# The end of a three-part kernel on one Trainium2 core: order of the last combine rows, place of their transposes, and form of the last product

## The chip, the cores and the metric

The program runs on one core of a Trainium2 chip. Its engines are TensorE (PE: products and transposes into PSUM), VectorE (DVE), ScalarE (ACT), GpSimd (POOL), SyncE (SP, which issues DMAs) and 16 DMA engines. The metric is the device time of one execution in microseconds (us).

## What is computed

Three parts follow one another: a linear attention, a mixture of experts in which every token goes to one expert with a fixed capacity, and a soft mixture of experts. The change touches the end of the third part alone. With x of shape 4352 x 128, 32 slots and 8 experts (F = 1024):

```python
logits = x @ phi
d = np.exp(logits - logits.max(0)); d /= d.sum(0) + 1e-09
slot_input = (d.T @ x).reshape(8, 4, 128)
for e in range(8):
    h = np.maximum(slot_input[e] @ w1[e], 0.0)
    slot_out[e] = h @ w2[e]
c = np.exp(logits - logits.max(1)); c /= c.sum(1) + 1e-09
return c @ slot_out.reshape(32, 128)
```

So every token needs its own row of c (a softmax over 32 slots), and the 32 slot outputs need the logits of all tokens.

## The kernel before, in words

The tokens stand in expert order in x2T (128 features by 4352 slots). The third part takes them in groups of four chunks of 128 slots while the second part still runs; the last group has three chunks and waits for the last expert. `soft_in` (L1277) does one group. Its inner functions are `logits` (PE, L1285), `largest` (DVE L1290 and L1292, ACT exponentials L1297 and L1299), `rows` (PE transposes of x2T L1305, ACT copy L1307), `weights` (PE L1313, ACT es L1317), `sums` (PE L1322, DVE S4 L1325) and `combine` (L1330 to L1352): an ACT copy, a PE transpose, six DVE operations with an ACT exponential between them make c_c, and POOL scatters one chunk at a time into cd in device memory, in token order (L1347). For the last group the order in the code is logits, largest, rows, soft_max, weights, sums and, last, combine (L1366 to L1375); the ACT copy of combine is put behind es by hand (`after`, L1334).

The program is written with a framework that orders the instructions of each engine itself, by their place in the code and by when their inputs are due; `after` adds an order by hand.

`soft_out` (L1447) then makes the slot outputs. slotP (L1459) holds the slot inputs. The first layer (L1469) is 16 products of 512 columns, each for 32 output columns, on the float32 weights M1; ACT and DVE apply the relu (L1473, L1474); eight transposes (L1479) and two copies (L1483, L1485) make HT. The second layer (L1493) is 64 products of 128 columns. A plain float32 product is two PE instructions, called passes here. Its generator `rows_back` (L1535) loads cd back in token order with three DMAs on SP (L1542 to L1544), transposes it in three batches (L1549) and splits each into c_hi, rounded to float32r (ACT, L1552), and the rest c_lo (DVE, L1553). The batches are issued ahead of steps 5, 6 and 7 of the second layer (BACK = 5, L1489). Y is copied out (L1497), Sel puts the slots in order (L1501), and SO is built: block-diagonal over four chunks (a quad), 128 x 512, one tile rounded to float32r and one with the rest (L1505 to L1515). The SO tiles were set to zero by POOL much earlier (L1409, 165.9 us). The last product has, for each of nine quads, three passes of 512 columns in float32r (L1518 to L1520); ACT or DVE copies the result (L1523, L1525), and SP stores it (L1528, 256 KB; the leftover quad 8, which comes first, L1531, 128 KB in pieces of 512 bytes).

`busy` (L1380) issues products of ones (wz) that nothing reads; BUSY holds their numbers, and BUSY[3] = 8 are issued ahead of the first layer (L1461).

Of the kernel before, what the change touches and what calls it, by code (L numbers as in the profile page):

```python
# [33 lines left out]
LS = 2.0 ** -40       # scale of the logits in the assignment  # L34
# [3 lines left out]
CE = 224  # slots of an expert that are filled early  # L38
CL = CAP - CE
TE = 24   # chunks whose tokens may go there  # L40
NE, NL = E * CE // 128, E * CL // 128
SPARE = 4608 + TE     # rows of x; further ones of c take slots that have no token
# [8 lines left out]
class K:  # L51
    def __init__(s, ctx, tc, I, out, dbg=None):
# [3 lines left out]
        s.nl = s.p.tile([128, NCH, 8], F32, name="nl")     # -logits * LS  # L56
        s.bad = s.p.tile([128, 1], I32, name="bad")
        s.badf = s.p.tile([128, 1], F32, name="badf")
        # of every slot, the row of its token for the gather, and the one that it is scattered to
# [11 lines left out]
    # ------------------------------------------------------------ constants  # L71
    def consts(s):
# [9 lines left out]
        # bm[p, h] = (p // 32 == h)  # L82
# [6 lines left out]
    # ------------------------------------------------------------ loads  # L89
# [3 lines left out]
    def after(s, b, a):  # L93
        """orders b behind a on their engine"""
        s.tc.add_manual_dep(b.ins, a.ins.name, mybir.DependencyInfo(
            mybir.DependencyClass.NoSync, mybir.DependencyReason.DATA), reason="order")

    def warm(s, n):
        """keeps the tensor engine busy until the first inputs are there, so that its clock is up"""
# [10 lines left out]
    def fill(s, key, ps):  # L110
        """keeps the tensor engine's clock up while it waits for what goes to this bank"""
# [30 lines left out]
    def x3(s, n, t):  # L142
        """[128 tokens, 4 heads, 32] of chunk t"""
# [4 lines left out]
    def xq(s, n, qd, h):  # L148
        """[128 tokens, (4 chunks, 32)] of a quad and head"""
# [4 lines left out]
    # ------------------------------------------------------------ S1, S2  # L154
    def decode(s):
# [11 lines left out]
        v.tensor_tensor(t[0], t[0], t[2], op=OP.bitwise_and)          # bits of the high part  # L167
# [5 lines left out]
        s.SS = c.tile([8, 2, 2, 4, 32], F32, name="SS")   # [r, hi|rem, S1|S2, rep, d]  # L173
# [4 lines left out]
    def weights(s):  # L178
        """block diagonal pieces of S1, S2 (transposed), and of P = S2^T S2"""
# [9 lines left out]
        hl = c.tile([128, 2, 64], F32, name="hl")        # (h, S1|S2, r)  # L189
# [14 lines left out]
    def pieces(s, r, n, pool=None):  # L204
        """r * 2^21 in two float16 parts, and r itself as bfloat16"""
# [34 lines left out]
    # ------------------------------------------------------------ K, V  # L240
    def ksplit(s, g):
        """K in float16: grid 2^-7, and the rest * 2^21 in two parts"""
# [35 lines left out]
    def phi(s, ph, ab, n):  # L278
        """products of the first n on the vector engine, of the others on Pool"""
# [8 lines left out]
    def add(s, b, h, c, w, x):  # L288
        """accumulates on columns c of a batch and head; the first one clears them all"""
# [29 lines left out]
    # ------------------------------------------------------------ G -> W, KV -> blocks  # L319
    def fin_tiles(s):  # L320
        nc = s.nc
        # pieces of W, block-diagonal over the chunks of a quad: batch b at 136 b, [(c', d), (h, c, r)];
        # so the leftover chunks find their blocks (c = b) 144 apart
        s.W = [s.a.tile([128, 576], dt, name="Wb%d" % i) for i, dt in enumerate((F16, F16, F16, BF))]
        # of a batch and a pair of heads u, rows (h % 2, f): block-diagonal KV, and KV @ w_gate, in columns
        # (u = 0: KV 64) (u = 0: 8) (u = 1: 8) (u = 1: KV 64)
# [6 lines left out]
    def Wof(s, x, qd, h):  # L333
        """the block of a quad and head"""
# [5 lines left out]
    def gfin(s, b):  # L340
        """W = S1 G P of a batch and every head, scaled by 2^-9, in pieces"""
# [3 lines left out]
        # Y = X + X^T, X = K0'R + R'R/2 (scaled by 2^21)  # L345
# [16 lines left out]
        # T1^T [d, (h, r)]  # L362
# [14 lines left out]
        # W^T [(c', d), (h, r)]  # L377
# [21 lines left out]
    def kvfin(s, b):  # L399
        """KV (scaled by 2^-9) of a batch, and KV @ w_gate, for pairs of heads"""  # L400
# [833 lines left out]
    def LO(s, e):  # L1234
        """the engines for the rests of an expert's weights"""
        return s.nc.vector, s.nc.gpsimd
# [488 lines left out]
```

## Time and profile before

| what | us |
|---|---|
| runs: lowest, median, highest of 3 | 316.4, 317.76, 329.15 |
| the profiled execution: span | 320.7 |
| its own time beside the span | not given by the page |
| PE busy | 278.7 (87%) |
| DVE, ACT, POOL busy | 215.0, 158.9, 153.4 |
| stores: first issue, last issue | 308.06, 315.09 |

The span goes from the first to the last instruction of the profiled execution. Busy time is a sum over instructions that may overlap: passes on PE are pipelined, and the share says little about the last 30 us, which are a tenth of it. They are read by windows and by the chain of work that ended last.

### The profile page before, as it was taken

The numbers are of one execution on the slowest core, as the hardware profiler recorded it, in microseconds if no ns is written. First come the engines' busy times: TensorE is split into PE (matmuls) and PEld (weight loads), VectorE is DVE, ScalarE is ACT, GpSimd is POOL, SyncE is SP. The second block draws the span as 40 slices with busy tenths as digits, with TensorE's granted clock in tenths as the row PEclk, the third lists the DMA queues.
The fourth block names the chain that finished last, engine by engine and source line by source line (L and its number), as shares of the span: only waits on it lengthen the run. The fifth ranks groups of instructions, "written<-read, shape, count | busy, mean of one in ns | idle before, by whom it ended". The sixth has DMA issues, their size and how long they took to land.

```text
span 320.7 us, 7215 instructions
## 1 busy us (share of the span) xinstructions
PE 278.7 (87%) x2687; PEld 231.0 (72%) x2697; DVE 215.0 (67%) x726; ACT 158.9 (50%) x457; POOL 153.4 (48%) x194
## 2 busy tenths in 40 slices
PE   7698659988999569999899999999969998999791
PEld 3576547866968548848798989788859997864570
DVE  8988987794593796456587888286655677644240
ACT  3326526543545372343855566468654876532230
POOL 6745434471170161077990505677884864443000
PEclk9759998996798755569999999999997999999977
DMA  6876864000010000128971000123146244200234
GB/s 158 237 252 208 260 192 141 2 36 35 4 65 33 35 1 0 68 82 251 330 231 42 8 3 11 41 52 97 47 145 195 76 141 138 68 8 10 72 132 156
DMA packets 34352, 32.58 MB, mean 102 GB/s; under 512 B 5740, under 2 KB 29284, under 8 KB 34308
## 3 DMA queue, kind: packets, MB, share of 16 engines
q1 hardware_dynamic: 26964, 24.43, 24.8%
q10 hardware_dynamic: 5024, 4.22, 4.6%
q0 software_dynamic: 2320, 3.38, 3.8%
q8 instruction: 23, 0.38, 0.5%
q14 instruction: 21, 0.17, 0.2%
HBM read 26.27 MB, written 5.75 MB: 100 GB/s over the span
## 4 chain that ended last, share of the span: by engine, by line
PE 63%; DVE 19%; POOL 5%; issue 4%; ACT 4%; DMA 2%; ACTq 1%; POOLq 0%; SPq 0%
PE py L1161 6%; PE ph L1151 6%; PE pt L534 4%; PE pt L481 4%; PE ph L1248 3%; PE py L1259 3%; PE ph L1249 3%; PE ph L1250 3%; PE py L1260 2%; PE py L1258 2%; PE acc L291 2%; PE mm L269 2%; PE ph L1171 2%; PE tp L534 2%; POOL cd L1347 2%
## 5 line engine op out<-in xcount | busy, mean ns | idle before, releaser
L1347 POOL DMA_INDIRECT cd<-c_c,ids x34 | 33.9, 998 | 28.5 <-DVE c_c L1345 18.4
L1123 POOL DMA_INDIRECT xg<-xd,idx x34 | 33.2, 977 | 12.7 <-issue 6.9
L1252 DVE SCALAR_TENSOR_TENSOR hl<-ph,hh 128x320 fp32r<-128x320 f32 x64 | 29.1, 486 | 13.5 <-ACT hh L1251 13.2
L1151 PE MATMUL ph<-xe,r 128*128 128x224 f32 x128 | 33.1, 358 | 1.8 <-ACT he L1153 1.5
L1161 PE MATMUL py<-he,r 128*128 128x224 f32 x128 | 34.0, 361 | 0.0
L1153 ACT ACTIVATE he<-ph 128x224 f32<-128x224 f32 x64 | 21.9, 357 | 22.6 <-PE ph L1151 18.9
L1251 ACT ACTIVATE hh<-ph 128x320 fp32r<-128x320 f32 x64 | 25.7, 449 | 7.9 <-PE ph L1250 7.8
L1151 PEld LDWEIGHTS ph<-xe,r 128*128 128x128 f32 x128 | 23.2, 190 | 2.8 <-ACT he L1153 2.1
L1161 PEld LDWEIGHTS py<-he,r 128*128 128x128 f32 x128 | 22.7, 191 | 1.5 <-issue 1.2
L1259 PE MATMUL py<-hh,w2l 128*128 128x320 f32 x64 | 20.5, 320 | 3.2 <-POOL w2l L1112 3.2
L1112 POOL TENSOR_TENSOR w2l<-r,w2h 128x512 fp32r<-128x512 f32 (+1 forms) x20 | 21.7, 1112 | 2.6 <-ACT w2h L1111 2.5
L1248 PE MATMUL ph<-xh,w1h 128*128 128x320 f32 x64 | 21.3, 341 | 0.3 <-ACT xh L1227 0.3
L534 PE MATMUL pt<-KX,phT 128*128 128x72 f32 x120 | 21.4, 327 | 0.0
L1260 PE MATMUL py<-hl,w2h 128*128 128x320 f32 x64 | 20.2, 316 | 1.2 <-DVE hl L1252 1.2
L1250 PE MATMUL ph<-xh,w1l 128*128 128x320 f32 x64 | 20.7, 324 | 0.0
L1249 PE MATMUL ph<-xl,w1h 128*128 128x320 f32 x64 | 20.4, 319 | 0.0
L1258 PE MATMUL py<-hh,w2h 128*128 128x320 f32 x64 | 20.3, 318 | 0.0
L534 PEld LDWEIGHTS pt<-KX,phT 128*128 128x128 f32 x120 | 19.3, 236 | 0.5 <-ACT phT L484 0.2
L467 POOL TENSOR_TENSOR Ahl<-al,l 128x128 f32<-128x128 f32 x9 | 5.7, 635 | 26.5 <-DVE al L466 23.5
L481 PE MATMUL pt<-ident,ph 128*128 128x128 f32 x72 | 16.1, 366 | 1.4 <-POOL ph L283 0.8
L283 POOL TENSOR_TENSOR ph<-kab 128x640 f32<-128x640 f32 x9 | 12.5, 1391 | 10.1 <-ACT kab L272 9.8
L1259 PEld LDWEIGHTS py<-hh,w2l 128*128 128x128 f32 x64 | 12.0, 188 | 4.2 <-POOL w2l L1112 3.6
(454 smaller groups left out, 838.8 us busy)
## 6 DMA issues: line engine op xcount, KB each, us to landing
r<-in_moe_w_dram SPq DMA_DIRECT2D x24, 512.0 KB, 5.0
r<-in_moe_w_dram ACTq DMA_DIRECT2D x8, 512.0 KB, 7.8
xd<-xt SPq DMA_DIRECT2D x9, 256.0 KB, 2.0
kb<-in_k_dram SPq DMA_DIRECT2D x4, 512.0 KB, 7.4
vb<-in_v_dram SPq DMA_DIRECT2D x4, 512.0 KB, 4.7
qb<-in_q_dram SPq DMA_DIRECT2D x4, 512.0 KB, 3.7
out_dram<-ot SPq DMA_DIRECT2D x8, 256.0 KB, 3.3
cd<-on POOLq DMA_DIRECT2D x1, 576.0 KB, 5.0
```

The source lines that it names most:

```text
L481: nc.tensor.transpose(ps[:, 128 * i:128 * i + 128], ph[:, 4 * i + 2 * u:4 * i + 2 * u + 2].rearrange("p h i j -> p (h i j)"), s.ident)
L534: s.lastx = nc.tensor.matmul(ps[:, o:o + 72], s.PHT[qd][:, u, 128 * (2 * k + i):128 * (2 * k + i) + 128], s.KX[:, s.batch(t), 72 * u:72 * ...
L1123: o = nc.gpsimd.indirect_dma_start(out=g, out_offset=None, in_=s.xd[0:rows], in_offset=bass.IndirectOffsetOnAxis(ap=s.idx[:, a:a + 1], axi ...
L1151: o = nc.tensor.matmul(ps, s.RW[e][0][:, 128 * k:128 * k + 128], X[:, CE * e:CE * e + CE], start=True, stop=True)
L1161: o = nc.tensor.matmul(Y[e], s.RW[e][1][:, k], Hs[e][:, k], start=(k == 0), stop=(k == 7))
L1248: nc.tensor.matmul(ps, w1h[:, f], xh, start=True, stop=False)
L1249: nc.tensor.matmul(ps, w1h[:, f], xl, start=False, stop=False)
L1250: nc.tensor.matmul(ps, w1l[:, f], xh, start=False, stop=True)
L1252: nc.vector.scalar_tensor_tensor(hl[:, k], ps, 0.0, hh[:, k].bitcast(F32), op0=OP.max, op1=OP.subtract)
L1258: nc.tensor.matmul(py, w2h[:, f], hh[:, k], start=(k == 0), stop=False)
L1259: nc.tensor.matmul(py, w2l[:, f], hh[:, k], start=False, stop=False)
L1347: st = nc.gpsimd.indirect_dma_start(out=s.cd, out_offset=bass.IndirectOffsetOnAxis(ap=s.ids[:, a:a + 1], axis=0), in_=cc[:, i], in_offset= ...
```

## The change

For the last group, combine comes first, right behind the logits, with no order by hand. BUSY[3] is 6. `rows_back` is an ordinary function that is called behind the second layer, Sel and the scaling of the slot outputs; it keeps the transposed c as plain float32 in one tile c_T. SO and its zeroing go. The slot outputs are written as so, 128 rows by two blocks of 128 columns; odd is 1 where a row belongs to the block. The last product is two plain float32 products per quad, rows 0 to 63 and rows 64 to 127, each 256 columns, into two PSUM tiles; ACT copies the first, DVE the second. The quads go in order 0 to 8. (The change also drops comments.)

```diff
@@ soft_in
         else:
+            combine(s.php.tile([128, CL], F32, name="ph"))
             x = largest()
             rows(x)
             s.busy(s.BUSY[0])
             s.soft_max(new)
-            x = weights(s.php.tile([128, CL], F32, name="ph"))
+            weights(s.php.tile([128, CL], F32, name="ph"))
             s.busy(s.BUSY[1])
             sums()
             s.busy(s.BUSY[2])
-            combine(bank(), x)
-    BACK = 5
-    BUSY = (2, 2, 4, 8, 3)
+    BUSY = (2, 2, 4, 6)
@@ slot_consts
-        zero = [nc.gpsimd.tensor_scalar(x, s.wz, 0.0, 0.0, op0=OP.mult, op1=OP.mult) for x in s.SO]
-        for o in zero + [nc.gpsimd.memset(s.slotP, 0.0)]:
-            s.after(o, s.lastp)
+        s.after(nc.gpsimd.memset(s.slotP, 0.0), s.lastp)
+        s.odd = s.p.tile([128, 2], F32, name="odd")
+        v.tensor_tensor(s.odd, s.bm[:, 0:2], s.bm[:, 2:4], op=OP.add)
@@ soft_out
-        back = s.rows_back()
         for k in range(8):
-            if k >= s.BACK:
-                next(back)
...
-        nc.scalar.activation(Y, py[:, 0:256].rearrange("p (g d) -> p g d", g=2), AF.Copy)
-        ch, cl = s.cT
+        nc.scalar.activation(Y[:, 0], py[:, 0:128], AF.Copy)
+        v.tensor_copy(Y[:, 1], py[:, 128:256])
...
-        sh, sl = tl("s_sh", [128, 128], F32R), tl("s_sl", [128, 128], F32R)
-        nc.scalar.activation(sh, po[:, 0:128], AF.Copy)
...
-        for i, qd in enumerate((8, 0, 1, 2, 3, 4, 5, 6, 7)):
-            pq = s.php.tile([128, 512], F32, name="po")
-            nc.tensor.matmul(pq, ch[:, qd], s.SO[0], start=True, stop=False)
-            nc.tensor.matmul(pq, cl[:, qd], s.SO[0], start=False, stop=False)
-            nc.tensor.matmul(pq, ch[:, qd], s.SO[1], start=False, stop=True)
+        so = tl("s_so", [128, 2, 128])
+        v.tensor_tensor(so, po[:, None, 0:128].to_broadcast([128, 2, 128]),
+                        s.odd[:, :, None].to_broadcast([128, 2, 128]), op=OP.mult)
+        s.rows_back()
+        for qd in range(9):
             ot = s.op.tile([128, 512], F32, name="ot")
-            if i % 2 == 0:
-                nc.scalar.activation(ot, pq, AF.Copy)
-            else:
-                v.tensor_copy(ot, pq)
+            for u in range(2):
+                pq = s.php.tile([128, 512], F32, name="po")
+                r, o = slice(64 * u, 64 * u + 64), ot[:, 256 * u:256 * u + 256]
+                nc.tensor.matmul(pq[:, 0:256], s.cT[r, qd], so[r].rearrange("p j d -> p (j d)"), start=True,
+                                 stop=True)
+                if u == 0:
+                    nc.scalar.activation(o, pq[:, 0:256], AF.Copy)
+                else:
+                    v.tensor_copy(o, pq[:, 0:256])
@@ rows_back
-            nc.scalar.activation(ch[:, g:g + n], o, AF.Copy)
-            v.tensor_tensor(cl[:, g:g + n], o, ch[:, g:g + n].bitcast(F32), op=OP.subtract)
-            yield
+            if n > 2:
+                nc.scalar.activation(s.cT[:, g:g + 2], o[:, 0:2], AF.Copy)
+                v.tensor_copy(s.cT[:, g + 2:g + n], o[:, 2:n])
+            else:
+                nc.scalar.activation(s.cT[:, g:g + n], o, AF.Copy)
```

## Rows read from the trace of the kernel before

**Rows 1.** Windows of the end: busy us (instructions) by engine, PE clock, DMA share, GB/s.

```profile
303.20:305.40 2.20, 0.74 (x5) 0.55 (x5) 0.74 (x4) 1.27 (x4) 0.00 (x0) 1.00 0.00 0
...
307.20:309.30 2.10, 2.10 (x6) 1.66 (x5) 0.69 (x1) 0.75 (x2) 0.00 (x0) 0.50 0.00 0
309.30:313.50 4.20, 4.18 (x18) 3.03 (x16) 2.07 (x3) 1.63 (x3) 0.00 (x0) 0.99 0.95 326
313.50:320.70 7.20, 0.00 (x0) 0.00 (x0) 0.01 (x1) 0.60 (x1) 0.00 (x0) 0.69 0.36 131
```

**Rows 2.** The chain of work that ended last: start us, us, what.

```profile
291.08 0.27 DVE c_c L1345
...
294.18 2.37 DMA cd<-c_c,ids
...
296.69 3.11 DMA c_tok<-cd
...
301.14 0.59 PE po L1549 x4
...
302.56 0.62 PE py L1493 x16
...
303.63 0.73 PE tp L1501 x4
...
305.37 0.50 PE po L1518
```

**Rows 3.** Timeline around the last group: start us, us, engine, line, operation, idle before.

```profile
285.04 0.45 PE L1384 MATMUL ph<-wz 128*128 128x320 bf16 x2
...
285.23 0.44 ACT L1264 ACTIVATE x2T<-py 128x320 f32<-128x320 f32 x1 [2.78 <-PE py L1260]
...
286.85 0.36 ACT L1297 ACTIVATE et<-tp,sN 96x128 f32<-96x128 f32 x1 [1.18 <-DVE sN L1292]
...
289.24 0.26 DVE L1337 TENSOR_REDUCE c_mx<-tp 128x3 f32<-128x96 f32 x1
...
289.96 1.46 PE L1384 MATMUL po<-wz 128*128 128x512 bf16 x6
...
290.56 0.19 DVE L1459 TENSOR_TENSOR slotP<-tp,s_rs 128x32 f32<-128x32 f32 x1
```

**Rows 4.** Timeline of the two layers on PE.

```profile
291.35 3.64 PE L1469 MATMUL po<-r,slotP 128*32 128x512 f32 x32
...
296.32 2.39 PE L1493 MATMUL py<-r,s_HT 128*32 128x128 f32 x80
```

**Rows 5.** Groups of instructions: count, busy us, mean ns, idle before and its releasers.

```profile
L456 DVE TENSOR_TENSOR qab<-mm,l 128x256 f32<-128x256 f32 x9 | 3.7, 416 | 2.5 <-ACT l L452 2.5
...
L1473 ACT ACTIVATE s_H<-po 128x256 f32<-128x256 f32 x2 | 0.8, 384 | 4.6 <-PE po L1469 4.6
...
L1505 ACT ACTIVATE s_sh<-tp 128x128 fp32r<-128x128 f32 x1 | 0.3, 277 | 0.8 <-PE tp L1501 0.8
...
L1409 POOL TENSOR_SCALAR SO<-wz 128x512 fp32r<-128x512 bf16 x2 | 1.4, 710 | 0.0
...
L1347 POOL DMA_INDIRECT cd<-c_c,ids x34 | 33.9, 998 | 28.5 <-DVE c_c L1345 18.4 <-issue 6.7 <-PE ph L1250 2.2
```

**Rows 6.** Timeline of PE amid the early experts, float32 of 224 columns.

```profile
188.35 0.54 PE L1151 MATMUL ph<-xe,r 128*128 128x224 f32 x2
188.72 0.54 PE L1161 MATMUL py<-he,r 128*128 128x224 f32 x2
```

**Rows 7.** Timeline of SP's queue at the stores.

```profile
308.06 0.66 SPq L1531 DMA_DIRECT2D out_dram<-ot  x1
...
313.53 1.46 SPq L1528 DMA_DIRECT2D out_dram<-ot  x1
```

**Rows 8.** Short windows at the stores; the last three columns are PE clock, DMA share, GB/s.

```profile
309.40:309.60 0.20, 0.20 (x3) 0.16 (x2) 0.00 (x0) 0.20 (x1) 0.00 (x0) 1.00 0.79 192
...
315.80:316.20 0.40, 0.00 (x0) 0.00 (x0) 0.00 (x0) 0.00 (x0) 0.00 (x0) 1.00 1.05 374
...
317.20:317.40 0.20, 0.00 (x0) 0.00 (x0) 0.00 (x0) 0.00 (x0) 0.00 (x0) 0.50 0.08 31
```

More of the change, by code (lines that the diff above doesn't have):

```diff
@@ L1328, in sums, with combine @@
                 v.tensor_copy(s.S4[:, 0:129], pS[:, 0:129])
-        def combine(pc, behind=None):
+        def combine(pc):
             l2 = tl("l2", [128, 128])
-            x = nc.scalar.activation(l2[:m], ps[:m, 0:128], AF.Copy)
-            if behind:
-                s.after(x, behind)
+            nc.scalar.activation(l2[:m], ps[:m, 0:128], AF.Copy)
             l3 = turn(l2, pc)
@@ L1502, in soft_out @@
                              start=(g == 0), stop=(g == 1))
-        sh, sl = tl("s_sh", [128, 128], F32R), tl("s_sl", [128, 128], F32R)
-        nc.scalar.activation(sh, po[:, 0:128], AF.Copy)
-        for j in range(4):
-            r, w = slice(32 * j, 32 * j + 32), slice(128 * j, 128 * j + 128)
-            if j < 2:
-                nc.scalar.activation(s.SO[0][r, w], sh[r], AF.Copy)
-            else:
-                v.tensor_copy(s.SO[0][r, w], sh[r])
-        v.tensor_tensor(sl, po[:, 0:128], sh.bitcast(F32), op=OP.subtract)
-        for j in range(4):
-            r, w = slice(32 * j, 32 * j + 32), slice(128 * j, 128 * j + 128)
-            v.tensor_copy(s.SO[1][r, w], sl[r])
-        for i, qd in enumerate((8, 0, 1, 2, 3, 4, 5, 6, 7)):
-            pq = s.php.tile([128, 512], F32, name="po")
-            nc.tensor.matmul(pq, ch[:, qd], s.SO[0], start=True, stop=False)
-            nc.tensor.matmul(pq, cl[:, qd], s.SO[0], start=False, stop=False)
-            nc.tensor.matmul(pq, ch[:, qd], s.SO[1], start=False, stop=True)
-            ot = s.op.tile([128, 512], F32, name="ot")
-            if i % 2 == 0:
-                nc.scalar.activation(ot, pq, AF.Copy)
-            else:
-                v.tensor_copy(ot, pq)
+        so = tl("s_so", [128, 2, 128])
[3 more added lines that the diff above has]
+        for qd in range(9):
+            ot = s.op.tile([128, 512], F32, name="ot")
+            for u in range(2):
[7 more added lines that the diff above has]
+                    v.tensor_copy(o, pq[:, 0:256])
             if qd < 8:
@@ L1538, in rows_back @@
         ct = s.sp.tile([128, NCH, 32], F32, name="c_tok", bufs=1)
-        ch, cl = [s.sp.tile([128, 9, 128], F32R, name=n, bufs=1) for n in ("c_hi", "c_lo")]
-        s.cT = ch, cl
+        s.cT = s.sp.tile([128, 9, 128], F32, name="c_T", bufs=1)
         nc.gpsimd.memset(ct[64:128, 32:36], 0.0)
@@ L1640, in rest @@
             s.slotP = xp.tile([128, 264], F32, name="slotP")
-            s.SO = [xp.tile([128, 512], F32R, name="SO%d" % i) for i in range(2)]
             s.sp = pool("sp", 2)
```

## The prediction

> **What bounds the kernel now.** I read the windows of the last 20 us first, then the chain of work that ended last, then the timeline around the places the change touches, and last the store windows. In the windows the reader is to see three limits one after the other [rows 1]. From 303.20 to 305.40 us PE works 0.74 us of 2.20 and waits for small copies. Then PE is busy without a gap, but its granted clock is 0.50 (the 1.2 GHz level) for part of the time. From 309.30 to 313.50 the DMA share is 0.95 at 326 GB/s: the stores are the limit, and in the 7.2 us after that nothing computes but the last copy. The chain names the causes [rows 2]. The last rows of c are ready at 291.35; their last scatter leaves at 294.18 and takes 2.37 us; the read-back leaves at 296.69 and has landed at 299.80. Only then can the transposes run that stand between parts of the second layer; its first 80 passes had ended at 298.71 [rows 4], and it ends at 303.18. Y, Sel and the block-diagonal SO take until 305.37, when the last product starts.
>
> **The change, part by part.** All sums are against the profiled execution, whose span is 320.7 us; the page gives no other time for it. That is 0.9% above the median of the runs shown, 317.76, and I carry differences over in microseconds.
>
> *Combine first.* It moves two ACT operations, one PE transpose, six DVE operations and three POOL scatters ahead of the largest logits, the transposes of x2T and the softmax weights; behind them on ACT now wait the exponentials and es, on DVE the steps to slotP, and for slotP PE's first layer. Today the six DVE operations run from 289.24 to 291.35, ACT's exponential between them [rows 2, 3]: in series that is 2.1 us. In the best case nothing is added: ACT had been idle 1.18 us before et, and the order on an engine is not the order of the code (wz products that the code issues behind the transposes of x2T run at 285.04, when x2T's last columns are not yet written [rows 3]), so short operations can fill gaps. I take 0.4 us added, nearer to the best case, because the wz products show slack on PE. Two wz products of 512 columns go (BUSY 8 to 6); six take 1.46 us and end where the first layer begins, 0.6 us after slotP is ready [rows 3, 4], so about 0.4 us comes back. First layer: still 291.35; bounds -0.5 and +2.1. POOL's three scatters move with c, some 2.5 us earlier; behind them on POOL is only the small fill of c_tok. SP's three loads follow at about 294.2 and land at about 297.3; behind them SP has only the stores, which are not due before 303. So c is there 3 us before a transpose that starts after 300. Even unmoved (299.80) it would be in time: if the scheduler delayed combine again, nothing would be lost there.
>
> *Transposes behind the second layer.* PE reaches the layer at 296.32 as now. 80 passes take 2.39 us, 0.030 each [rows 4]; all 128 in one run take 3.82 us: it ends at 300.14, 3.04 us earlier. If the scheduler pulled the transposes forward to before the data is there, at most the present wait of 1.1 us (298.71 to 299.80) stays.
>
> *Y, Sel, so.* Between the layer and Sel are 0.45 us [rows 2], of which the copy of 256 columns is 0.38 (as L1473 [rows 5]). Two engines with 128 columns each take 0.28 (L1505 [rows 5]): 0.35 in all, so Sel starts at 300.49 and, at 0.73 us [rows 2], ends at 301.22. The copies that make SO and its rest go; one DVE product of 128x256 out of PSUM replaces them, 0.42 us (L456 [rows 5]).
>
> *Nine transposes.* Four take 0.59 us in the chain [rows 2], so nine take 1.33 and end at 302.55. The DVE product (ready 301.65) and the first copies of c (0.38 on ACT, 0.42 on DVE, ready by 302.3) lie beside them. Cost on the path: 1.33 us, where the making of SO held PE for 1.0 (304.36 to 305.37 [rows 2]).
>
> *The last product.* Before, three passes of 512 columns of float32r per quad. After, a half is 64 rows by 256 columns of plain float32. Float32 takes two passes per product; 224 columns take 0.37 us for both, by the starts in the timeline [rows 6], so 256 columns take 0.43. If the two halves follow each other: 0.86 us a quad. If they run side by side in two halves of the rows: 0.43. No row shows two products on different rows. The nearest is the first layer: its 32 passes of 512 columns, on 32 output columns each, take 3.64 us [rows 4], 0.114 each, a quarter of what 512 columns of float32 take one after another; so products that fill the array only in part do run together here. I take 0.43 and keep 0.86. The Trainium skill, page TensorEngine Tiling, section Tiling Modes, says that tiles work independently, two of 64 rows among them, which would be 0.43; the packing by columns in the trace agrees, a packing by rows no run here shows. The copies are 256 columns on each engine, 0.38 and 0.42 us [rows 5], in step with 0.43. First store ready: 302.55 + 0.43 + 0.05 + 0.42 = 303.45, against 308.06: 4.6 us earlier.
>
> *Stores.* From then on they are the limit, since a quad is ready every 0.46 us and its store takes 0.70 (262 kB at 374 GB/s [rows 8]). Before, the first data moved 1.3 us after the first issue (308.06, and the share is 0.79 from 309.40 [rows 7, 8]). Eight stores are 5.6 us, the one of 131 kB in small pieces 0.68 at 192 GB/s (the window in which it moved [rows 8]). From the last data, about 317.3, to the end are 3.4 us. Sum: 303.45 + 1.3 + 6.28 + 3.4 = 314.4. One issue took 1.46 us on SP before [rows 7], and the last store waited for it; behind a queue that is some 2 us ahead such a pause is covered. Without that cover it costs 1 us.
>
> *Zeroing of SO.* Two POOL operations of 0.71 us go, far ahead of the end; I price them at nothing, since POOL waits 18.4 us for c before its scatters [rows 5]; the bounds are 0 and -1.4. The new odd is one DVE operation of two columns beside them, below 0.3 us by the nearest row, L1505's 128 columns.
>
> Sum: 320.7 - 314.4 = 6.3 us less. 317.76 - 6.3 = **311.5 us**. A measurement of this kernel tells about 2%, 6.4 us, from no change, so the forecast itself stands almost on that line.
>
> **The rivals.**
> *Halves in series.* PE becomes the bound again: 302.55 + 9 x 0.86 = 310.3, then copy 0.45, 1.3 to the data, 0.68, 3.4: 316.1, a gain of 4.6, so 313.2. For it: no row shows packing by rows. Against it: packing by columns.
> *The clock falls, halves side by side.* It went to 0.50 in the last product, behind a stretch with 0.74 us of work in 2.2, and was back at 1.00 by 309.40, so after at most 4.0 us of unbroken work [rows 1, 2, 8]. After the change PE idles 0.35 us around Y and works on Sel and the transposes for 2.1 us: less reason to fall, but not none. Price: 0.43 us on the first quad and 0.15 on each of the next three over the pace of the stores: 0.9 us, so 312.4.
> *Combine holds up slotP in full.* 2.1 us less the 0.4 that was counted: gain 4.6, so 313.2. Against it: the gaps and the order shown above.
> *Slower.* Halves in series and the clock at 0.50 through the whole product, because the pauses for copies never let it rise: 1.71 us a quad, 15.4 in all, 302.55 + 15.4 + 5.8 = 323.8, which is 3.1 us slower: 320.9. It decides from 1.37 us a quad (302.55 + 9 x 1.37 + 5.8 = 320.7). Against it: the clock came back within the last product before.
>
> **How the numbers follow.** Forecast 0.45, halves in series 0.18, clock 0.14, combine in full 0.12, slower 0.04, and 0.07 for gains beyond the forecast (transposes in the gap before Sel, a first layer 0.5 us earlier: gain 7.5 to 8). Own range of the forecast: 310.0 to 312.8. Faster by over 2% means below 311.4: near half of the forecast (0.21), the 0.07, and the part of the clock and combine cases in which other terms came out better (0.08): 0.36. Slower by over 2% means above 324.1, beyond even the slow rival: 0.03. Within 2%: 0.61. The range leaves out the slow rival and the far ends: 309.2 to 315.2.
>
> **What would show each step.** Right: the first scatter of the last c near 289; c_tok's loads on SP near 294; 128 passes of the second layer in 3.8 us without a gap; the two halves of a quad starting within 0.1 us of each other; a pair of copies every 0.46 us; DMA share near 1.0 for 6 us without a pause. Wrong: a first layer later than 292; product passes starting 0.21 us apart in one row; a granted clock of 0.50 after 303; stores that wait for SP. The forecast fails most if the first store is not ready by 304.5.

## The result and the profile after

| | kernel before | changed kernel |
|---|---|---|
| median of 20 runs each, us | 318.83 | 314.83 |
| lowest and highest, us | 315.47 to 330.23 | 309.94 to 323.27 |
| ratio to before | | 0.9846, 95% interval 0.9809 to 0.9884 |
| profiled execution: span, us | 320.7 | 315.8 |
| its own time, us | not given | 317.65 |

The ratio compares the faster executions of each kernel alone, since some of either fall in a slower state; the medians of all runs differ by 4.0 us. The ratio is 4.9 us of 318.83 (3.7 to 6.1): faster, but within the 2% that a measurement of this kernel tells from no change. The prediction was 6.3 us.

The two spans differ by 4.9 us as well, and 1.08 of that is not the change's: the last copy into x2T, from which all that was changed follows, starts at 284.15 us instead of 285.23. Ahead of it the change touches only the zeroing of SO on POOL (at 165.9 us in the kernel before) and odd (0.14 us at 9.5 us), and the shift is there before the zeroing: products of L1151 that stand at 164.32 us before stand at 162.20 after. Further executions below have it anywhere from 280.2 to 313.4. So I read each trace from the start of that copy, in the same six stretches as the prediction:

| stretch, us | before | predicted | after |
|---|---|---|---|
| last x2T copy to first layer | 6.12 | 6.12 | 6.28 |
| first layer to second layer | 4.97 | 4.97 | 6.63 |
| second layer | 6.86 | 3.82 | 4.16 |
| its end to the last product | 2.19 | 2.41 | 1.81 |
| product to first store issued | 2.69 | 0.90 | 1.24 |
| first store issued to the end | 12.64 | 10.98 | 11.53 |
| sum | 35.47 | 29.20 | 31.65 |

The chain of the changed kernel (start us, us, what) shows the same steps as [rows 2]:

```profile
284.15 0.45 ACT x2T L1264
...
290.98 2.12 DMA cd<-c_c,ids
...
293.24 3.12 DMA c_tok<-cd
...
296.50 0.41 PE po L1538 x2
296.91 0.22 PE po L1478 x2
297.13 2.85 PE py L1489 x97
...
300.14 1.08 PE py L1489 x31
301.22 0.58 PE po L1538 x4
...
303.03 1.14 PE po L1510 x8
```

c comes back earlier, as intended: its loads leave 9.09 us after the x2T copy (11.46 before). But two transposes of c_tok (L1538) stand in a place that the code does not give them: in front of the last two transposes of HT (L1478), and so ahead of the second layer. The timeline (start us, us, engine, line, operation, in brackets the idle time before it and its releaser) shows the price:

```profile
294.01 1.01 PE L1478 MATMUL po<-ident,s_H 128*128 128x128 f32 x6
...
296.50 0.41 PE L1538 MATMUL po<-ident,c_tok 128*128 128x128 f32 x2 [1.48 <-DMA c_tok<-cd]
...
296.75 0.38 PE L1478 MATMUL po<-ident,s_H 128*128 128x128 f32 x2
...
297.17 0.69 DVE L1484 COPY s_HT<-po 128x512 f32<-128x512 f32 x1 [2.19 <-PE po L1478]
```

PE stands for 1.48 us, since an engine works in its own order: behind the two that wait for memory are two that have their input, and behind those stand the layer and the copy of the second half of HT. The wait within the layer [rows 2, 4] has gone, and a wait in front of it has come.

The windows of the changed kernel (busy us by engine, then the granted clock, the DMA share and GB/s) answer to [rows 1] and [rows 8]:

```profile
295.02:296.50 1.48, 0.00 (x0) 0.03 (x1) 0.00 (x0) 0.28 (x1) 0.00 (x0) 1.00 0.81 301
...
297.06:301.22 4.16, 4.00 (x130) 3.64 (x130) 0.69 (x1) 0.00 (x0) 0.00 (x0) 1.00 0.02 4
...
303.03:304.27 1.24, 1.23 (x10) 0.83 (x10) 0.86 (x3) 0.58 (x3) 0.00 (x0) 1.00 0.00 0
...
305.20:311.40 6.20, 3.40 (x22) 2.27 (x20) 2.77 (x7) 2.39 (x7) 0.00 (x0) 1.00 1.01 359
311.40:313.20 1.80, 0.00 (x0) 0.00 (x0) 0.00 (x0) 0.00 (x0) 0.00 (x0) 0.89 0.05 7
313.20:315.80 2.60, 0.00 (x0) 0.00 (x0) 0.00 (x0) 0.00 (x0) 0.00 (x0) 0.50 0.04 13
```

The product runs at the full clock now (0.50 for 2.1 us before), the stores move for 6.2 us at a share of 1.01 without a pause, and behind them are 4.4 us (3.4 before) in which next to nothing moves.

### The profile page after: what moved, and what is told of

The parts are those of the page before. It is cut to its first block, busy times and chain, and to the rows that moved or that the text cites. A ratio compares the mean times of both kernels' runs of the same rounds, so it can differ in the third digit from the quotient of the medians.

```text
span 315.8 us, 7237 instructions
## 1 busy us (share of the span) xinstructions
PE 273.4 (87%) x2704; PEld 226.2 (72%) x2704; DVE 215.0 (68%) x726; ACT 158.3 (50%) x458; POOL 151.3 (48%) x192
## 4 chain that ended last, share of the span: by engine, by line
PE 61%; DVE 19%; POOL 6%; DMA 4%; issue 4%; ACT 3%; POOLq 0%; DVEq 0%; SPq 0%; ACTq 0%
PE py L1161 7%; PE ph L1151 7%; PE pt L534 4%; PE ph L1248 3%; PE py L1259 3%; PE ph L1250 3%; PE ph L1249 3%; PE pt L481 3%; PE py L1260 3%; PE py L1258 3%; DMA xg<-xd,idx 2%; DVE ph L283 2%; PE acc L291 2%; PE mm L269 2%; PE po L1510 2%
## 5 line engine op out<-in xcount | busy, mean ns | idle before, releaser
L1161 PE MATMUL py<-he,r 128*128 128x224 f32 x128 | 34.8, 369 | 0.0
L1151 PE MATMUL ph<-xe,r 128*128 128x224 f32 x128 | 34.0, 365 | 0.2 <-ACT xe L1144 0.2
L1151 PEld LDWEIGHTS ph<-xe,r 128*128 128x128 f32 x128 | 24.1, 196 | 0.7 <-ACT xe L1144 0.3
L1112 POOL TENSOR_TENSOR w2l<-r,w2h 128x512 fp32r<-128x512 f32 (+1 forms) x20 | 20.9, 1073 | 2.6 <-ACT w2h L1111 2.5
L534 PE MATMUL pt<-KX,phT 128*128 128x72 f32 x120 | 19.6, 308 | 0.0
L534 PEld LDWEIGHTS pt<-KX,phT 128*128 128x128 f32 x120 | 17.6, 219 | 0.5 <-ACT phT L484 0.2
L481 PE MATMUL pt<-ident,ph 128*128 128x128 f32 x72 | 14.9, 346 | 1.9 <-POOL ph L283 1.1
L1306 POOL MEMSET X<- 128x8 f32 x9 | 0.9, 111 | 31.6 <-PE tp L1322 19.0
```

The source lines that it names most:

```text
L534: s.lastx = nc.tensor.matmul(ps[:, o:o + 72], s.PHT[qd][:, u, 128 * (2 * k + i):128 * (2 * k + i) + 128], s.KX[:, s.batch(t), 72 * u:72 * ...
L1151: o = nc.tensor.matmul(ps, s.RW[e][0][:, 128 * k:128 * k + 128], X[:, CE * e:CE * e + CE], start=True, stop=True)
L1161: o = nc.tensor.matmul(Y[e], s.RW[e][1][:, k], Hs[e][:, k], start=(k == 0), stop=(k == 7))
```

## The experiments

My theory: the order that the framework gives the transposes takes back about 1.5 us, and the rest of the change does what was forecast. The rivals: the stores and the tail set the end, so the wait costs nothing; combine first is what gains, or what loses; the product gains only by its clock.

The kernels ran in three groups, each on one chip. On the first two chips the kernel before took 342.58 and 342.86 us, on the third 318.78, so ratios compare best within a group, and stretches from the x2T copy compare across all. The first group is e1_behind to e4_small_first, the second r_changed, e8, e7 and e5, the third r_before, e6, e9 and r_e1. The stretches are of one execution each. All executions in one table (us, from the timelines; stretches as above):

| kernel | to 1st layer | to 2nd | 2nd layer | to product | to store | to end | sum | ratio to before |
|---|---|---|---|---|---|---|---|---|
| before | 6.12 | 4.97 | 6.86 | 2.19 | 2.69 | 12.64 | 35.47 | |
| changed | 6.28 | 6.63 | 4.16 | 1.81 | 1.24 | 11.53 | 31.65 | 0.9846 |
| e1_behind | 6.35 | 4.97 | 3.70 | 1.94 | 1.24 | 11.94 | 30.14 | 0.9814 (0.9771 to 0.9857) |
| e2_combine_last | 6.22 | 5.67 | 3.70 | 2.34 | 1.27 | 11.56 | 30.76 | 0.9841 (0.9814 to 0.9869) |
| e3_same_rows | 6.35 | 7.83 | 4.89 | 1.84 | 1.62 | 13.18 | 35.71 | 0.9949 (0.9886 to 1.0011) |
| e4_small_first | 6.35 | 7.62 | 5.37 | 1.97 | 1.27 | 12.58 | 35.16 | 0.9900 (0.9843 to 0.9957) |
| r_changed | 6.31 | 7.74 | 4.97 | 1.84 | 1.23 | 11.63 | 33.72 | 0.9976 (0.9932 to 1.0019) |
| e8_staggered | 6.30 | 4.98 | 3.70 | 1.94 | 1.23 | 11.76 | 29.91 | 0.9842 (0.9769 to 0.9915) |
| e7_old_product | 6.67 | 4.97 | 3.70 | 3.36 | 2.34 | 12.35 | 33.39 | 1.0009 (0.9941 to 1.0077) |
| e5_no_branch | 6.35 | 7.67 | 5.22 | 1.84 | 1.23 | 8.70 | 31.01 | 0.9778 (0.9708 to 0.9847) |
| r_before | 6.12 | 4.97 | 6.86 | 2.19 | 3.16 | 12.32 | 35.62 | one run |
| e6_combine_alone | 6.59 | 7.03 | 6.89 | 2.24 | 2.25 | 12.21 | 37.21 | 1.0079 (1.0030 to 1.0129) |
| e9_two_banks | 6.28 | 4.97 | 3.70 | 1.64 | 1.33 | 11.57 | 29.49 | 0.9755 (0.9686 to 0.9824) |
| r_e1 | 6.28 | 4.97 | 3.70 | 1.95 | 1.23 | 11.56 | 29.69 | 0.9755 (0.9687 to 0.9823) |

### The transposes held behind the layer

```diff
-                nc.tensor.transpose(pt[:, 128 * i:128 * i + 128],
-                                    ct[:, 4 * (g + i):4 * (g + i) + 4].rearrange("p a x -> p (a x)"), s.ident)
+                s.after(nc.tensor.transpose(pt[:, 128 * i:128 * i + 128],
+                                    ct[:, 4 * (g + i):4 * (g + i) + 4].rearrange("p a x -> p (a x)"), s.ident), s.last2)
```

(s.last2 is the last pass of the second layer.)

> The changed kernel with one more ordering edge: all nine transposes of c_tok stand behind the last pass of the second layer (nothing else differs). Theory A: in the changed kernel two of them had been pulled in front of the last two transposes of HT, and PE stood 1.48 us for the loads of c_tok. Without that the second layer starts 11.2 to 11.5 us after the last x2T copy (12.91 in the changed kernel, 11.09 before), its 128 passes still take 4.0 to 4.2 us, and the time falls by 1.2 to 1.5 us: about 313.4 beside 314.8, ratio to before about 0.980. Theory B: the work only moves, since nine transposes instead of seven now lie between the layer and the product: that stretch grows from 1.81 to about 2.4 us and 0.9 us is left. Theory C: the stores and the end of the program set the time: no difference.

Measured: 0.9814, and 30.14 us from the x2T copy. The second layer starts 4.97 us behind the first as before the change, 11.32 us after the x2T copy, and its 128 passes take 3.70 us. The transposes fill the time around Y and Sel, so that stretch grows by 0.13 us alone: theory A, neither B nor C. The timeline of the same kernel in its second measurement, r_e1, has all eight HT transposes in one row and the layer in one piece:

```profile
300.86 1.47 PE L1478 MATMUL po<-ident,s_H 128*128 128x128 f32 x8
...
302.26 3.70 PE L1489 MATMUL py<-r,s_HT 128*32 128x128 f32 x128
...
305.89 0.66 PE L1538 MATMUL po<-ident,c_tok 128*128 128x128 f32 x4
```

### The changed kernel again

> The changed kernel itself, on the same chip as the three beside it. Both theories of e1_behind need it: if the wait for c_tok in front of the last two HT transposes is a matter of luck (1.48 us and the clock kept in the first profile, over 2 us and the clock at 0.64 to 0.71 in the second layer in two later ones), its profile again shows a second layer that starts 12.5 to 13.7 us after the last x2T copy. Ratio to before 0.985 to 0.990.

Measured: 0.9976 (0.9932 to 1.0019), weaker than expected: on this chip the change gains nothing that can be told. The second layer starts 14.06 us after the start of the x2T copy, outside the expected range, and 13.62 after its end, just inside; the expectation doesn't say from which it counts. Timeline, then windows:

```profile
316.53 0.55 PE L1538 MATMUL po<-ident,c_tok 128*128 128x128 f32 x2 [2.26 <-DMA c_tok<-cd]
```

```profile
317.43:319.40 1.97, 1.97 (x41) 1.79 (x44) 0.69 (x1) 0.00 (x0) 0.00 (x0) 0.50 0.00 0
319.40:322.40 3.00, 3.00 (x97) 2.74 (x90) 0.00 (x0) 0.00 (x0) 0.00 (x0) 0.89 0.03 5
```

Here PE waits for 2.26 us, and then the granted clock is 0.50 (the 1.2 GHz level) for the first 2 us of the layer, which takes 4.97 us instead of 3.70. Together that is 4.0 us against r_e1 (33.72 less 29.69), where the first profile of the changed kernel showed 1.96. The other three executions with this order (e3, e4 and e5) have layers of 4.89, 5.37 and 5.22 us, so the first profile was the mild case. The wait is longer there because c is back later: the loads leave 9.85 to 10.12 us after the x2T copy in these four, 9.09 in the first profile. The last scatter starts 0.3 to 0.4 us later, and it takes longer to land (2.12 us in the first profile, 2.78 in e4 and e5); why was not tried.

### Combine put back

```diff
-            combine(s.php.tile([128, CL], F32, name="ph"))
             x = largest()
...
             s.busy(s.BUSY[2])
+            combine(bank(), x)
```

(On e1_behind; the edge behind the softmax weights as before.)

> As e1_behind, and combine put back behind the softmax weights and sums, as before the change. Theory A: with all transposes behind the layer the way of c through memory is hidden even then: c_tok has landed about 14.6 us after the last x2T copy (as before), the layer ends about 15.4 us after it, so the time is that of e1_behind within 0.5 us, and the first layer starts up to 0.2 us earlier (6.1 after x2T instead of 6.28). Theory B: c comes back too late for the transposes: PE waits for c_tok behind the layer, the product starts 0.5 to 2 us later than in e1_behind, and the time is that much longer.

Measured: 30.76 us, 0.62 more than e1_behind and 1.07 more than its second measurement, r_e1; the ratios (0.9841 and 0.9814) have overlapping intervals. Theory B by its sign, at the lower end of its size. The timeline:

```profile
316.76 0.38 ACT L1474 ACTIVATE s_H<-po 128x256 f32<-128x256 f32 x1 [1.79 <-PE po L1480]
...
323.94 0.30 PE L1540 MATMUL po<-ident,c_tok 128*128 128x128 f32 x1 [0.56 <-DMA c_tok<-cd]
```

The ninth transpose, whose rows come with the last load, waits 0.56 us behind the layer; and ACT's second relu stands behind the first HT transposes, which starts the second layer 0.70 us later. Why ACT was held there was not tried, so the 0.6 to 1.1 us are not the wait for c alone. The first layer starts 0.13 us earlier than in e1_behind and 0.06 earlier than in r_e1, so combine first costs that much on the way to slotP.

### Combine first, alone

The mirror image: the kernel before with only the first part of the change.

```diff
+            combine(s.php.tile([128, CL], F32, name="ph"))
             x = largest()
...
             s.busy(s.BUSY[2])
-            combine(bank(), x)
```

> The kernel before with one part of the change: combine first. Three of the c_tok transposes now stand in front of the last two HT transposes, as two did in the changed kernel. Theory A: PE waits there for c_tok (loads issued 9.4 us after the last x2T copy, landed about 12.6), the second layer starts 12.5 to 13.7 us after x2T (10.66 before), its passes then run without the stops within (4.2 us, or 5 with the clock down), so the layer ends at 16.8 to 18.6 beside 17.5 before: no gain, between 0.7 us less and 1.2 us more, ratio 0.997 to 1.005. Theory B: the part is worth the wait that it was to remove, about 1 to 3 us: ratio 0.990 to 0.996.

Measured: 1.0079 (1.0030 to 1.0129), slower by 2.5 us, and 37.21 us from the x2T copy, 1.74 more than before. Theory A, beyond its upper end. The windows:

```profile
291.37:293.14 1.77, 0.00 (x0) 0.03 (x1) 0.00 (x0) 0.28 (x1) 0.00 (x0) 1.00 0.74 276
...
293.81:295.80 1.99, 1.99 (x44) 1.98 (x47) 0.69 (x1) 0.00 (x0) 0.00 (x0) 0.56 0.00 0
295.80:297.87 2.07, 2.07 (x45) 1.86 (x37) 0.00 (x0) 0.00 (x0) 0.00 (x0) 0.60 0.00 0
```

So this part brings the early transposes with it: three of them now stand ahead of the last HT transposes although the code has them in the middle of the second layer, PE waits 1.77 us, and the clock falls in the layer: its first 80 passes take 4.06 us where [rows 4] show 2.39. Alone, the part that was to shorten a wait makes one.

### The old product in the new order

```diff
-            if k >= s.BACK:
-                next(back)
...
+        for _ in s.rows_back():
+            pass
```

(On e6_combine_alone, with the edge of e1_behind.)

> The kernel before with two parts of the change: combine first, and the transposes behind the second layer (with the edge of e1_behind). The last product stays in three float32r passes with its block-diagonal inputs. Theory A: the layer ends 14.6 us after the last x2T copy (17.46 before), and the product's clock falls as before behind the copies that make its inputs (0.50 at first, 27 passes in about 8.1 us, end of the product about 25.5 after x2T): 2.0 to 2.5 us less than before, ratio 0.992 to 0.994, so the product is worth the larger part of what e1_behind gains. Theory B: the clock holds because PE no longer waits within the layer: 27 passes in 5.8 to 6.2 us, nearly as fast as the new product, and the gain is 4 us or more, ratio 0.988 or lower.

Measured: 33.39 us and a ratio of 1.0009 (0.9941 to 1.0077). Each theory has one half. The clock holds at 1.00 and the 27 passes take 6.8 us (longer than B's 5.8 to 6.2, shorter than A's 8.1), yet the part is only 2.1 us shorter than before (A). What is late is in the chain:

```profile
329.37 0.61 ACT c_hi L1551
...
330.00 1.49 DVE c_lo L1552 x3
...
331.51 0.22 DVE SO L1510
...
332.11 0.47 PE po L1517
```

DVE makes all nine c_lo first and then SO, and PE does nothing from 330.5 to 332.1. Before the change those operations lay beside the second layer. Against e1_behind, which has the same order of the work, the old end costs 3.25 us: 1.42 up to the product, 1.10 to the first store, 0.41 in the stores, and 0.32 ahead of the first layer (two wz products more). So in this order the new form of the end is worth more than its passes: the splits into hi and lo have gone from the way. What the old end would cost with the splits put elsewhere was not tried.

### Both halves on the same rows

```diff
+                r = slice(0, 64)
                 nc.tensor.matmul(pq[:, 0:256], s.cT[r, qd], so[r].rearrange("p j d -> p (j d)"), start=True,
```

> The changed kernel with both halves of a quad on rows 0 to 63; the second half's columns then come from the first half's slots, so that part of the output is left out. Theory A: in the changed kernel the two halves run at the same time because they lie on different rows; on the same rows the passes follow each other, about 0.22 us each, 0.86 us a quad, so the 36 passes take 7.7 us instead of 5.56, PE and no longer the stores sets the pace (0.70 us a store), and the end comes 0.5 to 1.5 us later. Theory B: the halves overlap for another reason (256 columns are simply short): the passes take 5.6 us as now and nothing changes.

Measured: the product takes 8.0 us and the first store is issued 0.39 us later; from the product to the end 14.80 us, against 12.86 in r_changed. The chains, first of the changed kernel (whose first 8 passes stand in a piece of their own, 1.14 us), then of this one:

```profile
304.17 4.44 PE po L1510 x27
```

```profile
327.40 8.02 PE po L1511 x36
```

All 36 passes follow each other, 0.22 us apart, as theory A has it. On different rows they take 5.56 us, and that is not PE's limit either: PE waits there for copies to free its PSUM tiles (0.41 us ahead of the third quad). So packing by rows works, and it is worth 1.9 us at the end. The time, 0.9949 (0.9886 to 1.0011), can't tell it from r_changed, which ran on another chip.

### The small store first

```diff
-        for qd in range(9):
+        for qd in (8, 0, 1, 2, 3, 4, 5, 6, 7):
```

> The changed kernel with quad 8 (the store in pieces of 512 bytes) first, as it was before the change, and quads 0 to 7 behind it. Theory A: the longer tail (4.4 us from the last data to the end, 3.4 before) comes from the small store being last: with it first, 3.4 us, and the time falls by 0.5 to 1.0 us. Theory B: the last store waits for the transfers of instructions behind the branch, whatever its shape: the tail stays 4.2 to 4.6 us and the time is the same within 0.4. Theory C: the small store at the front runs at half the rate while the stores behind it wait: 0.3 us longer.

Measured: from the first store's issue to the end 12.58 us, 0.95 more than in r_changed. The windows show where:

```profile
331.20:331.80 0.60, 0.60 (x7) 0.34 (x4) 0.25 (x1) 0.38 (x1) 0.00 (x0) 1.00 0.93 179
331.80:336.30 4.50, 2.14 (x14) 1.41 (x12) 1.88 (x5) 1.54 (x5) 0.00 (x0) 1.00 1.02 378
336.30:337.80 1.50, 0.00 (x0) 0.00 (x0) 0.00 (x0) 0.00 (x0) 0.00 (x0) 1.00 0.75 243
337.80:339.50 1.70, 0.00 (x0) 0.00 (x0) 0.00 (x0) 0.00 (x0) 0.00 (x0) 0.75 0.09 33
```

Theory C for the front, with 0.95 us instead of 0.3: the small pieces run there at 179 GB/s. Theory B for the tail (4.4 us from 337.8): large pieces at a share of 0.09 remain at the end as the small ones did, so it does not come from the shape of the last store. By this stretch the change's order is the better one; the times, on different chips (0.9900 beside 0.9976), don't show it.

### No branch at the end

```diff
-        with tc.If(nc.values_load(s.bad[0:1, 0:1], min_val=0, max_val=1) > 0):
-            with ExitStack() as st:
-                s.begin(st)
-                s.rest(s.reroute)
```

> The changed kernel without the block behind the branch at its end (the recomputation for a rare case; the inputs here do not take it); this part is left out. Theory A: behind the last product the engines jump over that block, and the transfers of instructions that follow (8 to 16 kB each, 310.8 to 313.6 in the trace of the changed kernel) hold up one DMA engine's share of the last store by 1.4 us (pieces until 313.07 where all others have ended by 311.7). Without the jump the last piece comes 7.1 to 7.5 us after the first store's issue (8.80 now), and the time falls by 1.3 to 2.5 us. Theory B: the lagging pieces have another cause: they stay, and the time is the same within 0.5 us.

Measured: 8.70 us from the first store's issue to the end, 2.93 less than in r_changed; 0.9778 beside 0.9976. The last data is 7.1 us behind the first issue, as theory A has it:

```profile
324.30:328.40 4.10, 3.42 (x23) 2.25 (x20) 2.80 (x7) 2.43 (x7) 0.00 (x0) 1.00 1.03 382
328.40:330.10 1.70, 0.00 (x0) 0.00 (x0) 0.00 (x0) 0.00 (x0) 0.00 (x0) 1.00 1.00 344
330.10:330.50 0.40, 0.00 (x0) 0.00 (x0) 0.00 (x0) 0.00 (x0) 0.00 (x0) 1.00 0.75 150
330.50:332.10 1.60, 0.00 (x0) 0.00 (x0) 0.00 (x0) 0.00 (x0) 0.00 (x0) 0.95 0.00 0
```

The stretch at a share of 0.05 (311.40 to 313.20 in the changed kernel) has gone, 1.8 us, and what follows the data is 1.6 us instead of 2.6. That the branch with its block costs this is shown; by what is not quite. In the changed kernel transfers of instructions start at 310.8 us, 0.6 us before nearly all of the data is through, and one of 16 KB runs from 310.9 to 312.3 beside the pieces that trickle; without the branch none is recorded from 320.6 us to the end (the first store is issued at 323.40). The DMA queues of the changed kernel from 309.5 to 313.2 us (packets, MB, share of 16 engines):

```profile
q1 hardware_dynamic: 511, 0.56, 48.8%
q8 instruction: 1, 0.02, 2.3%
q14 instruction: 3, 0.02, 1.6%
```

The Trainium skill, page "Runtime: NRT & Kernel Launch", section "Instruction fetch mechanics", says that a taken branch whose target lies outside what has been fetched forces a transfer before the engine goes on; transfers that are there with the branch and not without it agree with that. That they are what holds up the last pieces no run here isolates. The gain in the time (2.0%, 6.8 us, between two ratios whose intervals are 0.4% and 0.7% to either side) is more than these 2.9 us; in the two profiles 2.7 us lie behind the start of the x2T copy and 2.3 ahead of it, and the cause of the latter stays open.

### The product ahead of five transposes

```diff
+        back = s.rows_back()
+        next(back)
         for qd in range(9):
+            if qd == 2:
+                for _ in back:
+                    pass
```

(rows_back stops behind each batch, and its later batches stand behind the last pass of the product that was issued.)

> As e1_behind, and only the first four transposes ahead of the product; the other five stand behind its quads 0 and 1. Theory A: the product needs no more than quads 0 to 3, and PE has slack behind the stores (36 passes in 5.6 us, stores 6.3), so the product starts 0.6 to 0.8 us earlier than in e1_behind (16.52 after x2T: now 15.7 to 15.9) and the end comes as much earlier: ratio to before 0.977 to 0.980. Theory B: quad 2 waits for the five transposes and the stores run dry: the DMA share falls under 0.9 behind the second store, and at most 0.2 us is left of it.

Measured: 29.91 us, 0.23 less than e1_behind and 0.22 more than r_e1: nothing that can be told. The product starts 1.94 us behind the layer, as there, so it was not the transposes that it waited for; and theory B holds for the rest, as the windows show:

```profile
322.40:323.00 0.60, 0.60 (x7) 0.60 (x6) 0.54 (x2) 0.38 (x1) 0.00 (x0) 1.00 1.03 389
323.00:323.60 0.60, 0.60 (x8) 0.45 (x5) 0.23 (x1) 0.38 (x1) 0.00 (x0) 1.00 0.62 232
323.60:324.20 0.60, 0.60 (x7) 0.56 (x6) 0.59 (x2) 0.38 (x1) 0.00 (x0) 1.00 0.60 229
```

### Two banks for Y

```diff
-        py = s.pyp.tile([128, 272], F32, name="py")
+        py = [s.pyp.tile([128, 272], F32, name="py") for g in range(2)]
...
+            if g == 0:
+                nc.scalar.activation(s.cT[:, 0:2], o[:, 0:2], AF.Copy)
+                nc.scalar.activation(s.cT[:, 2:4], o[:, 2:4], AF.Copy)
+            elif g == 4:
+                v.tensor_copy(s.cT[:, 4:8], o)
```

(The order of Sel and the transposes is held by `after`.)

> As e1_behind, with the two halves of py in two tiles of PSUM (two banks), the first four c_T by ACT alone and the next four by DVE behind the product with odd, and Sel between the first four transposes and the other five. Theory A: in e1_behind the copy of Y's second half on DVE began only when ACT's had ended (0.31 us later), since both read one tile of PSUM, and the copy of c_T on DVE held up the product with odd: without both, the two Y copies start within 0.05 us, and the product starts 0.25 to 0.45 us earlier (1.94 us behind the layer's end in e1_behind: now 1.5 to 1.7), the end as much earlier. Theory B: the second Y copy waits for another reason and stays 0.3 us behind; the nine transposes are the limit, and the product starts at 1.9 as now. In the time itself either is at the limit of what can be told: ratio 0.978 to 0.982.

Measured: the product starts 1.64 us behind the layer (1.95 in r_e1), the sum is 29.49 (29.69), and the times are the same: 0.9755 both. Theory A, though the three edits in it were not tried one by one. The timelines, e1_behind and then this kernel:

```profile
327.95 0.28 ACT L1493 ACTIVATE s_Y<-py 128x128 f32<-128x128 f32 x1 [3.88 <-PE py L1489]
...
328.26 0.29 DVE L1494 COPY s_Y<-py 128x128 f32<-128x128 f32 x1 [3.28 <-ACT s_Y L1493]
```

```profile
297.01 0.28 ACT L1495 ACTIVATE s_Y<-py 128x128 f32<-128x128 f32 x1 [3.66 <-PE py L1489]
...
297.23 0.29 DVE L1496 COPY s_Y<-py 128x128 f32<-128x128 f32 x1 [2.97 <-PE py L1489]
```

With one tile DVE is released by ACT's copy, with two by PE; the copies overlap then, though not within the 0.05 us that I expected, since DVE's half is finished later by PE. The Trainium skill, page "PSUM — Partial Sum Buffer", section "PSUM bank collisions raise a hardware error", says that no two engines may be on one bank and group of 32 partitions at once, reads included, so that software has to keep them apart. The two releasers agree with it; what an overlap in one bank would do no run here shows.

### Before, and the version behind the layer, once more

> The kernel before, for its trace on the chip of the three runs beside it (where it takes 342 us, against 318.8 on the first). If the loss of those chips lies ahead of the changed part, from the last x2T copy to the end it takes 35 us as on the first chip, with the layer's end 17.5 us after that copy and the first store's issue at 22.4. If the part itself is slower there (c comes back later, the clock falls in the second layer), the layer ends at 18 or later.

Measured: this group's chip turned out to be one on which the kernel before takes 318.78 us, so whether the part is slower on the other two can't be told from it; e1_behind (30.14) and r_e1 (29.69) say that it hardly is. What it does show: the first four stretches repeat to 0.01 us and the sum is 35.62 beside 35.47. Between e1_behind and r_e1 the sums differ by 0.45, nearly all of it in the stores (11.94 and 11.56). So differences of a microsecond between the sums are real, and smaller ones ahead of the stores.

> e1_behind again beside e9_two_banks. If its gain over the changed kernel (0.9976 on the chip of r_changed) is real, ratio 0.980 to 0.987, and 29.5 to 29.9 us from the last x2T copy to the end; if the first measurement was luck, 0.990 or higher.

Measured: 0.9755 (0.9687 to 0.9823), better than expected, and 29.69 us from the start of the copy, 29.25 from its end. e1_behind and the changed kernel never ran in one group. The nearest pair on one chip is e8, which has the edge in a further order, and r_changed: 0.9842 (0.9769 to 0.9915) beside 0.9976 (0.9932 to 1.0019). Across chips it is 0.9814 beside 0.9976, and 0.9755 beside 0.9846, where the intervals overlap a little. So the sums (30.14 and 29.69 beside 31.65 and 33.72) carry the comparison, and the ratios agree with them. With one edge more than the change e1_behind takes 310.96 us where the kernel before takes 318.78.

## Why the prediction was right, and where it was not

The direction was right and the size 1.4 us too good (the median, 314.83 us, lies inside the wide range and above the forecast's own 310.0 to 312.8), and one step has most of the blame. That the number came so near is partly luck: of the 4.9 us the stretches of the first profile show 3.8, and on the chip of r_changed the same kernel gained 0.8 us (between 2.3 gained and 0.7 lost). r_e1 is the change as I had forecast it, with the transposes where the code puts them: 29.69 us against the 29.20 of my sum. The changed kernel has 31.65 in its mild case and 33.72 in the other.

The step that failed is this one, word for word: "If the scheduler pulled the transposes forward to before the data is there, at most the present wait of 1.1 us (298.71 to 299.80) stays." I had seen the danger and bounded it by the old place of the wait, within the layer with 80 passes ahead of it. The framework put the transposes ahead of the layer, where only the first six HT transposes stood before them, and so the wait is 1.48 us in the first profile and 2.26 to 2.49 in the four others with this order, and in those four the layer behind it ran below the full clock, for another 1.2 to 1.7 us (layers of 4.89 to 5.37 instead of 3.70). That also makes "PE reaches the layer at 296.32 as now" wrong: the layer starts 1.82 us later, counted from the x2T copy. The trace of before held the warning that I used for another point: the order on an engine is not that of the code [rows 3]. And I gave no chance to the rival that the change doesn't do what it says.

The other steps:

- *Combine first.* The first layer was to stay where it was; it came 0.16 us later. The two terms of 0.4 us that were to cancel come out as 0.47 added (e6, with the eight wz products kept) and 0.31 given back. The rival with slotP held up in full (1.7 us) is wrong. c was to be back 2.5 us earlier; the loads left 2.37 us earlier in the first profile and 1.3 to 1.6 in the four others. What I had not seen: combine first is also what moved the transposes (e6), so the part alone costs 1.7 us; with the order held it is worth 0.6 to 1.1 (e2).
- *Second layer.* Forecast 3.82 us in one run, measured 3.70 with the order held, 4.16 without in the first profile. There the granted clock was 1.00; what the 0.46 us went to was not looked into.
- *Y, Sel, so and the transposes.* 2.41 forecast, 1.81 to 1.95 measured, mainly from two errors of opposite sign. The two Y copies do not run side by side from one tile (0.31 us apart; e9), and the nine transposes do not stand on the path for 1.33 us: most of them lie in PE's gaps around Y and Sel. PE waits for so and c_T, not for its own work (e8).
- *The quad.* Side by side was right: passes on the same rows take 8.0 us, on different rows 5.56 (e3). The first store came 1.24 us behind the product's start instead of 0.90: I had charged the last pass with the distance to the next, 0.22 us, and not with its own 0.38:

```profile
L1510 PE MATMUL po<-s_so,c_T x36: 376/376/480, 303.0 to 308.2; 64*128 64x256 f32 x36
```

  (Group of that line in the changed kernel: minimum, median and maximum ns.) Copy and issue make up the rest. The rival "halves in series" is refuted, and so is the clock's fall in the product; the clock fell in the second layer instead, where no rival of mine had it.
- *Stores.* 6.28 us of data forecast, 6.2 measured. The first data moved about 0.75 us after the issue (1.3 forecast), and the tail was 4.4 us (3.4). The two nearly cancel: 11.53 against 10.98. e5 puts 2.9 us of the stretch down to the branch, and e4 shows that the order of the stores is not the cause of the tail. The kernel before has the branch too, so why the tail grew by 1.0 us stays open.

Where the gain came from, then, by the sums: the order of combine and transposes, held by hand, 2.1 us (35.47 to e7's 33.39); the new form of the end 3.3 to 3.7 us more (to e1_behind and r_e1); and 1.5 to 4.0 us of that are given back by two transposes in the wrong place (31.65 and 33.72 less 30.14 and 29.69).

## What to carry to other kernels

Where a framework orders an engine's instructions by when it believes their inputs due, making a slow input earlier can move its consumer ahead of work that is ready; look up the order in the new program, or fix it with an edge, before you price a wait as gone. Bound a wait by every place at which the waiting instruction may end up, and count what is queued behind it there. And read a change from a landmark just ahead of it: here the same program ended 30.1 and 29.7 us behind the landmark in two executions (e1_behind and r_e1), while the landmark itself stood at 312.9 and 291.0 us.

## What was not expected of the hardware

- The second layer's clock: behind 1.48 us in which PE did nothing it stayed at 1.00 (first profile of the changed kernel), as the product's did behind 1.60 us (e7); behind 1.77 (e6) and 2.26 us (r_changed) it was 0.50 to 0.60 for 2 to 4 us. In the kernel before it fell behind 2.2 us in which PE worked for 0.74 [rows 1]. A short wait can cost more than itself.
- The end of a program with a branch over a large block costs 2.9 us more than without it, though the block is never entered: 1.8 us in which the last pieces of a store trickle at a share of 0.05, and 1.0 us more behind them.
- The same program takes 318 us on some chips and 342 on others, with the stretch from the last x2T copy nearly the same; the difference lies ahead of it and was not looked into.
